# Channel attention on one core: seven packed blocks in place of five, with a shorter ring of row buffers

## The chip, the cores and the metric

The kernel runs on one core of a Trainium2 chip. The metric is device time in microseconds (us). Three runs of the kernel before gave 734.32, 734.56 and 734.57 us; the median, 734.56, is the time before.

## What is computed

The input x is one image of 384 x 384 points with 384 channels in bfloat16, and w1 (384 x 96) and w2 (96 x 384) are small matrices.

```python
xf = x.reshape(B, H * W, C)
gap = jnp.mean(xf, 1)
gmp = jnp.amax(xf, 1)
h_a = gap @ w1;  h_a = h_a * (h_a > 0)
h_m = gmp @ w1;  h_m = h_m * (h_m > 0)
scale = sigmoid(h_a @ w2 + h_m @ w2)
return x * scale[:, None, None, :]
```

Mean and maximum of each channel run over all points, so every point has to be read before the first result can be written. The 113.2 MB of x don't fit into the core's memory. What isn't kept there has to be read a second time.

## The kernel before, in words

A "row" here is one point for each of the 128 partitions: 128 x 384 x 2 bytes = 98,304 bytes (96 KB). The image has TOT = 1152 rows. The kernel divides them into blocks (`take`, from L85 on), and three kinds of block need not be read again:

- **Kept rows.** Three blocks of 44 rows stay in the three slots of `ring` (132 rows), 21 in `held`, 12 in `up`, and a few in PSUM and `acc`.
- **Packed rows.** PACKED = 5 blocks of 32 rows are each packed into 24 rows of `room`. A block has four parts of G = 8 rows: parts 0, 1 and 2 lie in `homes[i]`, part 3 in `fourth[i]`, which is one of two places in `held`.
- **All others** pass through the ring and are read again: `AGAIN`, 800 rows.

**First pass** (loop over `steps`, L317 to L351). SyncE issues the loads in the order of the list `steps`. Each load into the ring goes to the next of three slots, and waits on SyncE's queue until the slot's earlier rows have been used by VectorE (running maximum, L315, in pieces of 6 and 5 rows by HALVES) and by TensorE (sums over the points, L260). All later loads stand behind it. For a packed block ScalarE tests the four parts (L283, L286), TensorE combines them in two halves (L297, 24 matmuls each, into one region of PSUM, `words`), and ScalarE copies each half back (L303, L304). The second half can't start before L304 of the first. In TensorE's order the second half stands after the sums of the first slot that follows the block (`if k == 0`). The list `BETWEEN` gives the loads between two packed blocks, `PASSING` those after the last one, `STAYING`, `LAST_UP` and `LAST_HELD` the pieces of the kept blocks. L347 copies eight early rows into PSUM.

**Between the passes** the scale of each channel is worked out (L355 to L392).

**Second pass.** First the kept rows are multiplied by the scale on VectorE (`multiply`, L397) and stored from ScalarE's queue (`put`). As their stores end, the ring's 132 rows are used as four places of 33 rows, into which SyncE reads blocks of `AGAIN` (`read_into`, L479). Then come 25 turns, counted from 0. Each turn:

1. multiplies a place on VectorE,
2. issues its store from ScalarE (`store`, L473),
3. lets SyncE read the next block into the place as soon as that store has ended,
4. emits a portion of the unpacking (`some`).

The generator `unpack` yields an assumed time for each VectorE instruction: 0.5 for a `tensor_scalar` (L430), 0.9 for `mix` (L434), 1.7 for the multiply of a part, and 0.0 for a byte copy on ScalarE (L440). `some` takes from it until a portion of CHUNK = 4.5 is used up. A block has two halves. Each half has eight VectorE instructions and then six copies on ScalarE; the second half starts by writing the scratch `f`, which the copies of the first half read, and the four multiplies of the block come after all copies. Portions begin in turn 1; blocks 0 to 3 are done by turn 21, block 4 is unpacked in the last turns. Every engine works through its own list in the order of the program, so ScalarE's stores and copies stand in one queue.

Unpacking makes 32 rows of 24, so the fourth part needs a place of its own (`homes_d`): in `held`, `up`, `acc` and in a part of the ring that the last turns don't use. All packed rows are stored in the last turns and after them.

Of the kernel before, what the change touches and what calls it, by code (L numbers as in the profile page):

```python
# [27 lines left out]

SLOT = 44
SLOTS = 3
PLACE = 33
G = 8
PACKED = 5
PSUM_ROWS = 8
LATE_ROWS = 6
BANK_ROWS = 2
# [1 line left out]
HELD_ROWS = 21  # L40
A = 11
HALVES = ((0, 6), (6, 11))
UP_ROWS = 12

FIRST_LOAD = 4
BETWEEN = ((22, 44, 44), (44, 44, 44), (44, 44, 40), (40, 40, 38), (38, 38, 36))
PASSING = (30, 32, 30, 28, 26, 22, 18, 14)
STAYING = ((20, 16, 8), (16, 14, 14), (12, 11, 11, 10))
LAST_UP = (8, 4)
LAST_HELD = (6, 5, 5, 5)  # L50

AGAIN = (33,) * 23 + (24, 17)
FIRST_STORES = ((1, 2, 3, 4, 4, 6, 8, 8, 8), (8, 8, 9, 9, 10), (10, 12, 22))
HELD_STORES = (7, 7, 7)
FIRST_READS = ((8, 8, 8, 9),)
ACC_STORES_AT = 3
EARLY = 4
FROM_TURN = 1
CHUNK = 4.5
TEST_SCALE = 0.031187  # L60
SUM_TAIL = 4
# [4 lines left out]
def kernel(  # L66
# [33 lines left out]
    def take(n):  # L100
        nonlocal at
        at += n
        return at - n, n
# [1 line left out]
    ps_block = take(PSUM_ROWS)  # L105
    beside = take(BANK_ROWS + A)
    packed_block = take(GP * PACKED)
    up_block = take(UP_ROWS)
    held_block = take(sum(LAST_HELD))
    stay = [(take(SLOT), s) for s in range(NS)]  # L110
# [32 lines left out]
    ring = xpool.tile([P, SLOT * NS, C], BF16, name="ring")  # L143
    slots = [ring[:, SLOT * i:SLOT * (i + 1), :] for i in range(NS)]
    places = [ring[:, PLACE * i:PLACE * (i + 1), :] for i in range(SLOT * NS // PLACE)]
    room = xpool.tile([P, 3 * G * PACKED + UP_ROWS, C], BF16, name="room")
    spare = room[:, 3 * G * PACKED, :]
    up = room[:, 3 * G * PACKED:, :]
# [53 lines left out]
    def fill(*parts):  # L202
        nonlocal n_slot
        j = 0
        for block, lo, hi in parts:
            steps.append(("load", block, slots[n_slot % NS][:, j:j + hi - lo, :], lo, hi))
            j += hi - lo
        n_slot += 1

    def whole(block):  # L210
# [19 lines left out]
    turned = []  # L230
    for (block, s), pieces in zip(stay, STAYING):
        s = n_slot % NS
        turned.append((block, s))
        cuts = [sum(pieces[:j]) for j in range(len(pieces) + 1)]
        for lo, hi in zip(cuts, cuts[1:]):
            steps.append(("load", block, slots[s][:, lo:hi, :], lo, hi))
        n_slot += 1
    stay = turned
    for block, buf, pieces in ((up_block, up, LAST_UP), (held_block, held, LAST_HELD)):
# [123 lines left out]
    n = A  # L363
# [9 lines left out]
        acc_pieces.append((lo, hi))  # L373

    def move_late(lo, hi):
        nc.vector.tensor_copy(out=late[:, lo:hi, :].bitcast(U32), in_=up[:, lo:hi, :].bitcast(U32))
        nc.sync.dma_start(out=up[:, lo:hi, :], in_=rows_of(xr, refill)[:, lo:hi, :])

    move_late(0, 2)
    for q0, part_ps in tp_ps:  # L380
# [20 lines left out]
    def put(block, buf, pieces, lo=0):  # L401
        j = 0
        for m in pieces:
            rows = buf[:, j:j + m, :]
            multiply(rows, rows)
            nc.scalar.dma_start(out=rows_of(orr, block)[:, lo + j:lo + j + m, :], in_=rows)
            j += m
# [4 lines left out]
            nc.scalar.dma_start(out=acc_rows(orr, lo, hi), in_=acc[:, lo:hi, :])  # L412


    turns = len(AGAIN)
    beside_last = [places[t % len(places)][:, AGAIN[t]:, :] for t in (turns - 2, turns - 1)]
    homes_d = [held[:, 0:G, :], held[:, G:2 * G, :], up[:, 0:G, :], acc[:, 0:G, :], beside_last[0][:, 0:G, :]]
    HG = G // 2
    f, m = up[:, G:G + HG, :], held[:, 2 * G:2 * G + HG, :]
    t = acc[:, G:G + HG // 2, :].rearrange("p n c -> p (n c)").bitcast(U8)  # L420

    def unpack(i):
# [20 lines left out]
        def nibbles_to_bytes(v):  # L443
            yield scalars(m, v, 3, ALU.logical_shift_right, 0x0101, ALU.bitwise_and)
            yield scalars(m, m, float(0x8F), ALU.mult, 0.0, ALU.add)
            yield mix(v, v, 0x3F3F, ALU.bitwise_xor, ALU.bitwise_xor, m)

        for h in range(2):
            a, b, w, d = (p[:, h * HG:(h + 1) * HG, :] for p in (*(part(i, r) for r in range(3)), homes_d[i]))
            yield scalars(f, w, 4, ALU.logical_shift_right, 0x0F0F, ALU.bitwise_and)  # L450
            yield scalars(w, w, 0x0F0F, ALU.bitwise_and, 0, ALU.bitwise_or)
            yield from nibbles_to_bytes(f)
            yield from nibbles_to_bytes(w)
            yield move(low(d, U8), high(b, U8))
# [6 lines left out]
            multiply(rows, rows)  # L461
            yield 1.7

    def work(blocks):
        for i in blocks:
            yield from unpack(i)

    def some(todo, us):
        while us > 0:
            us -= next(todo, us)  # L470

    def store(buf, block, lo):
        nc.scalar.dma_start(out=rows_of(orr, block)[:, lo:lo + buf.shape[1], :], in_=buf)  # L473
# [17 lines left out]
    (b0, s0), (b1, s1), (b2, s2) = sorted(stay, key=lambda b: b[1])  # L491
    k = ACC_STORES_AT
    put(b0, slots[s0], FIRST_STORES[0][:k])
    put_acc()
    j = sum(FIRST_STORES[0][:k])
    n = SLOT - j
    rest = slots[s0][:, j:, :]
    put(b0, rest, FIRST_STORES[0][k:], j)
    put(held_block, held, HELD_STORES)
    read_into(places[0])  # L500
    put(b1, slots[s1], FIRST_STORES[1])
    put(up_block, up[:, LATE_ROWS:, :], (UP_ROWS - LATE_ROWS,), LATE_ROWS)
    put(refill, up[:, 0:LATE_ROWS, :], (LATE_ROWS,))
    read_into(places[1])
    put(b2, slots[s2], FIRST_STORES[2])
# [4 lines left out]
    early, last = work(range(EARLY)), work(range(EARLY, PACKED))  # L510
    half = 3 * G * 2
    d_at = 3 * G * PACKED
    for turn in range(turns):
        b, buf = order.pop(0)
        multiply(buf[:, 0:b[1], :], buf[:, 0:b[1], :])
        j = turn - (turns - 3)
        if j in (0, 1):
            store(room[:, j * half:(j + 1) * half, :], packed_block, j * half)
        elif j == 2:
            store(held[:, 0:2 * G, :], packed_block, d_at)  # L520
            store(homes_d[2], packed_block, d_at + 2 * G)
            store(homes_d[3], packed_block, d_at + 3 * G)
# [9 lines left out]
    some(last, 1000.0)  # L532
    j = 0
    for block, lo, rows in ((ps_block, 0, kept_ps[:, 0:PSUM_ROWS, :]), (up_block, 0, late), (beside, 0, kept_b)):
        n = rows.shape[1]
        multiply(beside_last[1][:, j:j + n, :], rows)
        store(beside_last[1][:, j:j + n, :], block, lo)
        j += n
    store(homes[4], packed_block, 2 * half)
    store(homes_d[4], packed_block, d_at + 4 * G)  # L540
# [37 lines left out]
```

## Time and profile before

| | |
|---|---|
| Median of three runs | 734.56 us |
| The profiled execution's own time | 733.96 us |
| Its span, first to last instruction | 732.2 us |
| Read from HBM, written | 193.71 MB, 113.25 MB |
| Busy: VectorE, ScalarE, TensorE | 541.4, 247.6, 160.3 us |
| Last maximum of the first pass ends | 271.5 us |
| First multiply by the scale | 277.07 us |
| Turn 0, turn 1, turn 2 start | 315.73, 329.62, 354.11 us |
| Block 0 to 3 unpacked | 336.3 to 550.8 us |
| Turn 22 starts | 654.77 us |

The page of the profile cuts the span into 40 slices of 18.3 us. In a row such as DVE (VectorE) or ACT (ScalarE) a digit is the busy share of a slice in tenths; the row GB/s is what the DMA engines moved. A line of the waits names who waited at which line of the kernel, for whom, and then the microseconds in total, the number of times and the longest. A line of the timeline has the start, the microseconds, engine, line, operation, output<-input, shapes and count, and in brackets the idle time before it with what ended it.

### The profile page before, as it was taken

What the parts mean: (1) busy time and instruction counts of PE and PEld (TensorE: products, weight loads), DVE (VectorE), ACT (ScalarE), POOL (GpSimd) and SP (SyncE); (2) the same over time, 40 slices, a digit from 0 to 9 for tenths busy, and PEclk for the clock granted to TensorE, in tenths of its full rate; (3) what the DMA queues carried; (4) which work ended last, traced back from release to release, by engine and by line L of the source; (5) the groups of instructions that cost most, each with busy time, mean ns of one, the idle gap of its engine ahead of it and who ended that gap; (6) DMA issues with size and microseconds to landing.
All of it is one profiled execution on the core that took longest, in us unless ns stands there. A gap on an engine that the chain in (4) does not pass through costs nothing.

```text
span 732.2 us, 3394 instructions
## 1 busy us (share of the span) xinstructions
PE 160.3 (22%) x1195; PEld 59.9 (8%) x1195; DVE 541.4 (74%) x398; ACT 247.6 (34%) x170; POOL 0.7 (0%) x6
## 2 busy tenths in 40 slices
PE   5375758384654550000000000000000000000000
PEld 1121213131211130000000000000000000000000
DVE  4399999999999999956368869798665543456450
ACT  6969697989200000000251440700530000002700
POOL 0000000000000000000000000000000000000000
PEclk9797979797855555555555555555555555555555
DMA  9999999999999979999999999999999999999997
GB/s 380 436 435 429 422 430 433 426 431 427 417 428 419 422 277 374 398 425 441 428 432 428 432 432 433 431 433 431 433 432 432 435 429 439 428 431 439 432 424 297
DMA packets 21409, 307.18 MB, mean 420 GB/s; under 512 B 2736, under 2 KB 3472, under 8 KB 9616
## 3 DMA queue, kind: packets, MB, share of 16 engines
q1 hardware_dynamic: 12896, 193.71, 62.4%
q10 hardware_dynamic: 8496, 113.25, 36.3%
q8 instruction: 9, 0.15, 0.1%
q14 instruction: 8, 0.07, 0.0%
HBM read 193.71 MB, written 113.25 MB: 419 GB/s over the span
## 4 chain that ended last, share of the span: by engine, by line
DVE 40%; DMA 38%; ACT 12%; issue 4%; PE 1%; ACTq 0%; SPq 0%; DVEq 0%
DMA ring<-in_x_dram 18%; DVE acc L315 16%; DVE ring L397 16%; DMA out_dram<-ring 14%; DMA room<-in_x_dram 5%; ACT room L440 3%; DVE room L397 3%; ACT held L283 2%; DMA held<-in_x_dram 2%; ACT held L286 2%; ACT held L440 2%; ACT acc L440 2%; DVE held L430 1%; DVE held L397 1%; PE kept_ps L297 1%
## 5 line engine op out<-in xcount | busy, mean ns | idle before, releaser
L397 DVE TENSOR_TENSOR ring<-ring,scale_bc 128x12672 bf16<-128x12672 bf16 (+12 forms) x43 | 193.5, 4524 | 81.3 <-DMA ring<-in_x_dram 79.3
L315 DVE TENSOR_TENSOR acc<-acc,ring 128x1920 bf16<-128x1920 bf16 (+4 forms) x184 | 205.4, 1191 | 1.0 <-DMA ring<-in_x_dram 1.0
L260 PE MATMUL bank_a<-ring,small 128*1 128x512 bf16 (+2 forms) x744 | 75.3, 458 | 51.8 <-DMA ring<-in_x_dram 51.8
L397 DVE TENSOR_TENSOR room<-room,scale_bc 128x3072 bf16<-128x3072 bf16 (+1 forms) x18 | 29.9, 1708 | 39.6 <-ACT room L440 39.6
L286 ACT ACTIVATE held<-held 128x3072 uint8<-128x3072 uint8 x20 | 57.1, 2856 | 0.6
L440 ACT COPY ring<-room 128x1536 uint8<-128x1536 uint8 x4 | 5.7, 1473 | 140.8 <-DVE ring L397 140.8
L440 ACT COPY held<-room 128x1536 uint8<-128x1536 uint8 x8 | 11.4, 1472 | 122.3 <-DVE ring L397 122.3
L283 ACT ACTIVATE held<-room,held 128x3072 uint8<-128x3072 int8 x15 | 42.8, 2856 | 23.6 <-DMA room<-in_x_dram 23.3
L440 ACT COPY room<-room 128x1536 uint8<-128x1536 uint8 x24 | 35.0, 1473 | 26.7 <-DVE ring L397 26.4
L260 PEld LDWEIGHTS <-small 128*1 128x1 bf16 x873 | 29.3, 93 | 129.6 <-issue 110.2
L297 PE MATMUL kept_ps<-room,scale_bc 128*128 128x512 fp8e4 (+1 forms) x90 | 30.4, 456 | 39.3 <-ACT room L304 29.1
L440 ACT COPY acc<-room 128x1536 uint8<-128x1536 uint8 x14 | 20.4, 1468 | 42.7 <-DVE ring L397 42.7
L270 ACT COPY w_sb<-bank_a 65x128 f32<-65x128 f32 x2 | 0.5, 262 | 77.6 <-PE bank_a L260 77.1
L315 DVE TENSOR_TENSOR acc<-acc,room 128x1920 bf16<-128x1920 bf16 (+4 forms) x26 | 26.5, 1078 | 0.0
L430 DVE TENSOR_SCALAR room<-room 128x1536 uint16<-128x1536 uint16 x20 | 11.2, 558 | 18.3 <-ACT room L440 17.9
L297 PE MATMUL kept_ps<-room,w_sb 128*128 128x512 fp8e3 (+1 forms) x60 | 21.1, 439 | 0.0
L297 PE MATMUL kept_ps<-held,room 128*128 128x512 fp8e4 (+1 forms) x60 | 19.9, 417 | 0.0
L434 DVE SCALAR_TENSOR_TENSOR room<-room,held 128x768 uint32<-128x768 uint32 x20 | 19.2, 958 | 0.7
L303 ACT COPY room<-room 128x1536 uint8<-128x1536 uint8 x10 | 14.7, 1468 | 2.7 <-PE kept_ps L297 2.7
L440 ACT COPY room<-acc 128x1536 uint8<-128x1536 uint8 x10 | 14.7, 1474 | 0.3
L260 PE MATMUL bank_a<-room,small 128*1 128x512 bf16 x99 | 10.7, 456 | 18.3 <-DMA room<-in_x_dram 18.3
L303 ACT COPY room<-held 128x1536 uint8<-128x1536 uint8 x10 | 14.7, 1470 | 0.0
(65 smaller groups left out, 155.0 us busy)
## 6 DMA issues: line engine op xcount, KB each, us to landing
out_dram<-ring ACTq DMA_DIRECT2D x23, 3168.0 KB, 25.6
ring<-in_x_dram SPq DMA_DIRECT2D x22, 3168.0 KB, 26.2
ring<-in_x_dram SPq DMA_DIRECT2D x7, 4224.0 KB, 21.9
ring<-in_x_dram SPq DMA_DIRECT2D x3, 3840.0 KB, 22.3
ring<-in_x_dram SPq DMA_DIRECT2D x3, 3648.0 KB, 22.7
room<-in_x_dram SPq DMA_DIRECT2D x4, 2304.0 KB, 27.6
out_dram<-room ACTq DMA_DIRECT2D x2, 4608.0 KB, 39.1
ring<-in_x_dram SPq DMA_DIRECT2D x2, 2880.0 KB, 15.1
```

The costliest lines, as they stand in the source:

```text
L260: nc.tensor.matmul(sum_ps[q * QP:q * QP + 1, 0:g * P], lhsT=ones_bf[:, 0:1], rhs=rows[:, k:k + g, q * P:(q + 1) * P], start=(done + k == 0 ...
L270: nc.scalar.copy(out=s_sb[r % 2], in_=sum_ps[:, r * P:(r + 1) * P])
L283: nc.scalar.activation(out=tested, in_=high(part(i, r), I8), func=ACT.Square, bias=test_bias, scale=TEST_SCALE,)
L286: nc.scalar.activation(out=tested, in_=tested, func=ACT.Square, bias=minus4, accum_out=tests[:, 4 * i + r:4 * i + r + 1],)
L297: nc.tensor.matmul(words[:, c:c + BANK], lhsT=weights[2 * r + k], rhs=high(part(i, r), dt)[:, half * n + c:half * n + c + BANK], start=(r ...
L303: nc.scalar.copy(out=high(part(i, r), U8)[:, span], in_=low(part(i, r + 2), U8)[:, span])
L315: nc.vector.tensor_tensor(out=out_, in0=in0, in1=in1, op=ALU.max)
L397: nc.vector.tensor_tensor(out=dst, in0=src, in1=scale_bc.unsqueeze(1).to_broadcast([P, n, C]), op=ALU.mult)
L430: nc.vector.tensor_scalar(out=u16(dst), in0=u16(src), scalar1=s1, scalar2=s2, op0=op0, op1=op1)
L434: nc.vector.scalar_tensor_tensor(out=u32(dst), in0=u32(src), scalar=both(s), in1=u32(other), op0=op0, op1=op1)
L440: nc.scalar.copy(out=dst, in_=src)
```

## The change

- PACKED goes from 5 to 7. `room` keeps 3 x 8 x 7 = 168 rows; `up` is gone, and the refilled rows of the first pass's end now lie at the start of `held`.
- The ring has 96 rows in place of 132. In the first pass it has three slots of 31 rows (the block kept in the last slot has 34), in the second four places of 24 rows.
- `BETWEEN` has four loads between two packed blocks, of 26 or 27 rows (10 for the first). The second half of a packed block's matmuls stands after the second of them (`if k == 1`). Three passing blocks follow in place of eight.
- 784 rows are read again, in 33 turns.
- Unpacking begins in turn 0 and takes all seven blocks with the same portions of 4.5. Blocks 0 and 1 are stored as soon as each is unpacked. After block 1, its home of 24 rows is used as a fifth place of the ring.
- Four more `homes_d` lie in places that were used before: block 2's in `held` 0 to 8, which held block 1's, block 3's in `held` 8 to 16, which held block 0's, and those of blocks 5 and 6 in block 0's home. From block 2 on the scratch `f` lies there too.

```diff
-SLOT = 44
+SLOT = 31
+RING = 96
-PLACE = 33
+PLACE = 24
-PACKED = 5
+PACKED = 7
-BETWEEN = ((22, 44, 44), (44, 44, 44), (44, 44, 40), (40, 40, 38), (38, 38, 36))
-PASSING = (30, 32, 30, 28, 26, 22, 18, 14)
-STAYING = ((20, 16, 8), (16, 14, 14), (12, 11, 11, 10))
-LAST_UP = (8, 4)
+BETWEEN = ((10, 27, 27, 27),) + ((26, 26, 26, 26),) * 6
+PASSING = (26, 23, 20)
+STAYING = {1: (16, 15), 2: (13, 11, 10), 0: (9, 8, 7, 7)}
-AGAIN = (33,) * 23 + (24, 17)
-FIRST_STORES = ((1, 2, 3, 4, 4, 6, 8, 8, 8), (8, 8, 9, 9, 10), (10, 12, 22))
-HELD_STORES = (7, 7, 7)
-FIRST_READS = ((8, 8, 8, 9),)
+AGAIN = (24,) * 32 + (16,)
+FIRST_STORES = ((1, 2, 3, 4, 5, 5, 5, 6), (8, 8, 8, 7), (9, 11, 14))
+HELD_STORES = (7, 8)
+FIRST_READS = ((6, 6, 6, 6),)
-EARLY = 4
-FROM_TURN = 1
...
-            if k == 0:
+            if k == 1:
                 steps.append(("pack", i, 1))
...
-    homes_d = [held[:, 0:G, :], held[:, G:2 * G, :], up[:, 0:G, :], acc[:, 0:G, :], beside_last[0][:, 0:G, :]]
+    homes_d = [held[:, G:2 * G, :], held[:, 0:G, :], held[:, 0:G, :], held[:, G:2 * G, :], acc[:, 0:G, :]]
+    homes_d += [room[:, 0:G, :], room[:, G:2 * G, :]]
...
+        f = room[:, 2 * G:2 * G + HG, :] if i > 1 else acc[:, 0:HG, :]
...
-    def work(blocks):
-        for i in blocks:
+    def work():
+        for i in range(PACKED):
             yield from unpack(i)
+            if i < 2:
+                store(homes[i], packed_block, 3 * G * i)
+                store(homes_d[i], packed_block, d_at + G * i)
+            if i == 1:
+                read_into(homes[1])
...
+    after = [
+        [(room[:, step:2 * step, :], step)],
+        [(room[:, 2 * step:3 * step, :], 2 * step)],
+        [(held[:, 0:2 * G, :], d_at + 2 * G), (homes_d[4], d_at + 4 * G), (room[:, 0:2 * G, :], d_at + 5 * G)],
+    ]
     for turn in range(turns):
         b, buf = order.pop(0)
         multiply(buf[:, 0:b[1], :], buf[:, 0:b[1], :])
...
+        if turn >= turns - len(after):
+            for rows, lo in after[turn - turns + len(after)]:
+                store(rows, packed_block, lo)
         store(buf[:, 0:b[1], :], b, 0)
         read_into(buf)
-        if FROM_TURN <= turn < turns - 4:
-            some(early, CHUNK)
-        elif turn == turns - 4:
-            some(early, 1000.0)
-        elif turn > turns - 4:
-            some(last, CHUNK)
+        if turn == turns - 4:
+            last = buf
+        some(todo, CHUNK if turn < turns - len(after) - 1 else 1000.0)
```

More of the change, by code (lines that the diff above doesn't have):

```diff
@@ L42 @@
 HALVES = ((0, 6), (6, 11))
-UP_ROWS = 12
 FIRST_LOAD = 4
-BETWEEN = ((22, 44, 44), (44, 44, 44), (44, 44, 40), (40, 40, 38), (38, 38, 36))
-PASSING = (30, 32, 30, 28, 26, 22, 18, 14)
-STAYING = ((20, 16, 8), (16, 14, 14), (12, 11, 11, 10))
-LAST_UP = (8, 4)
+BETWEEN = ((10, 27, 27, 27),) + ((26, 26, 26, 26),) * 6
+PASSING = (26, 23, 20)
+STAYING = {1: (16, 15), 2: (13, 11, 10), 0: (9, 8, 7, 7)}
 LAST_HELD = (6, 5, 5, 5)
-AGAIN = (33,) * 23 + (24, 17)
-FIRST_STORES = ((1, 2, 3, 4, 4, 6, 8, 8, 8), (8, 8, 9, 9, 10), (10, 12, 22))
-HELD_STORES = (7, 7, 7)
-FIRST_READS = ((8, 8, 8, 9),)
+AGAIN = (24,) * 32 + (16,)
+FIRST_STORES = ((1, 2, 3, 4, 5, 5, 5, 6), (8, 8, 8, 7), (9, 11, 14))
+HELD_STORES = (7, 8)
+FIRST_READS = ((6, 6, 6, 6),)
 ACC_STORES_AT = 3
-EARLY = 4
-FROM_TURN = 1
 CHUNK = 4.5
@@ L107 @@
     packed_block = take(GP * PACKED)
-    up_block = take(UP_ROWS)
     held_block = take(sum(LAST_HELD))
-    stay = [(take(SLOT), s) for s in range(NS)]
+    stay = {s: take(sum(pieces)) for s, pieces in STAYING.items()}
     refill = take(LATE_ROWS)
@@ L142 @@
     held = nc.alloc_sbuf_tensor_at("held", [P, HELD_ROWS, C], BF16, offset=RING_BYTES).ap()
[L143 to L148, printed above, removed]
+    ring = xpool.tile([P, RING, C], BF16, name="ring")
+    slots = [ring[:, SLOT * i:SLOT * i + stay[i][1], :] for i in range(NS)]
+    places = [ring[:, PLACE * i:PLACE * (i + 1), :] for i in range(RING // PLACE)]
+    spare = ring[:, SLOT * NS, :]
+    room = xpool.tile([P, 3 * G * PACKED, C], BF16, name="room")
     homes = [room[:, 3 * G * i:3 * G * (i + 1), :] for i in range(PACKED)]
@@ L207, in fill @@
             j += hi - lo
+            assert j <= SLOT
         n_slot += 1
@@ L229 @@
     fill(whole(refill), whole(passing[-1]))
[L230 to L239, printed above, removed]
+    assert n_slot % NS == next(iter(stay))
+    parts_left = [(stay[i], slots[i], pieces) for i, pieces in STAYING.items()] + [(held_block, held, LAST_HELD)]
+    for block, buf, pieces in parts_left:
         for j, m in enumerate(pieces):
@@ L375, in move_late @@
     def move_late(lo, hi):
-        nc.vector.tensor_copy(out=late[:, lo:hi, :].bitcast(U32), in_=up[:, lo:hi, :].bitcast(U32))
-        nc.sync.dma_start(out=up[:, lo:hi, :], in_=rows_of(xr, refill)[:, lo:hi, :])
+        nc.vector.tensor_copy(out=late[:, lo:hi, :].bitcast(U32), in_=held[:, lo:hi, :].bitcast(U32))
+        nc.sync.dma_start(out=held[:, lo:hi, :], in_=rows_of(xr, refill)[:, lo:hi, :])
     move_late(0, 2)
@@ L415 @@
     turns = len(AGAIN)
-    beside_last = [places[t % len(places)][:, AGAIN[t]:, :] for t in (turns - 2, turns - 1)]
-    homes_d = [held[:, 0:G, :], held[:, G:2 * G, :], up[:, 0:G, :], acc[:, 0:G, :], beside_last[0][:, 0:G, :]]
+    homes_d = [held[:, G:2 * G, :], held[:, 0:G, :], held[:, 0:G, :], held[:, G:2 * G, :], acc[:, 0:G, :]]
+    homes_d += [room[:, 0:G, :], room[:, G:2 * G, :]]
     HG = G // 2
-    f, m = up[:, G:G + HG, :], held[:, 2 * G:2 * G + HG, :]
+    m = held[:, 2 * G:2 * G + HG, :]
     t = acc[:, G:G + HG // 2, :].rearrange("p n c -> p (n c)").bitcast(U8)
@@ L462, in unpack @@
             yield 1.7
-    def work(blocks):
-        for i in blocks:
+    d_at = 3 * G * PACKED
+    def work():
+        for i in range(PACKED):
             yield from unpack(i)
+            if i < 2:
[3 more added lines that the diff above has]
+                read_into(homes[1])
     def some(todo, us):
@@ L489, in read_into @@
             order.append((b, buf))
-    (b0, s0), (b1, s1), (b2, s2) = sorted(stay, key=lambda b: b[1])
     k = ACC_STORES_AT
-    put(b0, slots[s0], FIRST_STORES[0][:k])
+    put(stay[0], slots[0], FIRST_STORES[0][:k])
     put_acc()
     j = sum(FIRST_STORES[0][:k])
[L496 to L499, printed above, removed]
+    put(stay[0], slots[0][:, j:, :], FIRST_STORES[0][k:], j)
+    put(held_block, held[:, LATE_ROWS:, :], HELD_STORES, LATE_ROWS)
+    put(refill, held[:, 0:LATE_ROWS, :], (LATE_ROWS,))
     read_into(places[0])
-    put(b1, slots[s1], FIRST_STORES[1])
-    put(up_block, up[:, LATE_ROWS:, :], (UP_ROWS - LATE_ROWS,), LATE_ROWS)
-    put(refill, up[:, 0:LATE_ROWS, :], (LATE_ROWS,))
+    put(stay[1], slots[1], FIRST_STORES[1])
     read_into(places[1])
-    put(b2, slots[s2], FIRST_STORES[2])
+    put(stay[2], slots[2], FIRST_STORES[2])
     read_into(places[2])
@@ L509 @@
     bad = nc.values_load(flag, engines=(ENG.SP, ENG.Activation, ENG.DVE))
-    early, last = work(range(EARLY)), work(range(EARLY, PACKED))
-    half = 3 * G * 2
-    d_at = 3 * G * PACKED
+    todo = work()
+    step = 3 * G * 2
+    after = [
[3 more added lines that the diff above has]
+    ]
     for turn in range(turns):
@@ L515 @@
         multiply(buf[:, 0:b[1], :], buf[:, 0:b[1], :])
[L516 to L522, printed above, removed]
+        if turn >= turns - len(after):
+            for rows, lo in after[turn - turns + len(after)]:
+                store(rows, packed_block, lo)
         store(buf[:, 0:b[1], :], b, 0)
         read_into(buf)
-        if FROM_TURN <= turn < turns - 4:
-            some(early, CHUNK)
-        elif turn == turns - 4:
-            some(early, 1000.0)
-        elif turn > turns - 4:
-            some(last, CHUNK)
+        if turn == turns - 4:
+            last = buf
+        some(todo, CHUNK if turn < turns - len(after) - 1 else 1000.0)
     assert not again and not order
-    some(last, 1000.0)
     j = 0
-    for block, lo, rows in ((ps_block, 0, kept_ps[:, 0:PSUM_ROWS, :]), (up_block, 0, late), (beside, 0, kept_b)):
+    for block, lo, rows in ((ps_block, 0, kept_ps[:, 0:PSUM_ROWS, :]), (held_block, 0, late), (beside, 0, kept_b)):
         n = rows.shape[1]
-        multiply(beside_last[1][:, j:j + n, :], rows)
-        store(beside_last[1][:, j:j + n, :], block, lo)
+        multiply(last[:, j:j + n, :], rows)
+        store(last[:, j:j + n, :], block, lo)
         j += n
-    store(homes[4], packed_block, 2 * half)
-    store(homes_d[4], packed_block, d_at + 4 * G)
+    store(homes[PACKED - 1], packed_block, 3 * G * (PACKED - 1))
     with tc.If(bad != 0):
```

## The prediction

> **What bounds the kernel now.** I read the slices first, then the waits, then VectorE's and ScalarE's timelines, turn by turn.
>
> ```profile
> DVE  4399999999999999956368869798665543456450
> ACT  6969697989200000000251440700530000002700
> ...
> GB/s 380 436 435 429 422 430 433 426 431 427 417 428 419 422 277 374 398 425 441 428 432 428 432 432 433 431 433 431 433 432 432 435 429 439 428 431 439 432 424 297
> ```
>
> The transfers are the bound almost everywhere: some 430 GB/s outside the turn between the passes. In the first pass VectorE is full too. In the second it is half empty on average, which hides this:
>
> ```profile
> DVE ring L397 <- DMA ring<-in_x_dram: 79.3, 11, 12.4
> ...
> DVE room L397 <- ACT room L440: 39.6, 5, 9.1
> ...
> DVE room L430 <- ACT room L440: 17.9, 5, 5.0
> ```
>
> While a block is unpacked VectorE also waits for ScalarE's byte copies: 57.5 us for five blocks. Three turns in the timeline of VectorE:
>
> ```profile
> 354.11 6.76 DVE L397 TENSOR_TENSOR ring<-ring,scale_bc 128x12672 bf16<-128x12672 bf16 x1 [12.43 <-DMA ring<-in_x_dram]
> 365.82 1.16 DVE L430 TENSOR_SCALAR room<-room 128x1536 uint16<-128x1536 uint16 x2 [4.95 <-ACT room L440]
> ...
> 371.13 6.75 DVE L397 TENSOR_TENSOR ring<-ring,scale_bc 128x12672 bf16<-128x12672 bf16 x1
> 386.94 5.09 DVE L397 TENSOR_TENSOR room<-room,scale_bc 128x3072 bf16<-128x3072 bf16 x3 [9.05 <-ACT room L440]
> 391.95 6.75 DVE L397 TENSOR_TENSOR ring<-ring,scale_bc 128x12672 bf16<-128x12672 bf16 x1
> ```
>
> A turn is the multiply of one place (6.75 us for 33 rows), then a portion of unpacking. The second turn here lasts 391.95 - 371.13 = 20.8 us, although nothing in it waits for a transfer. Turns that only wait for transfers (starts at 564.82 to 654.77, six of them) are 14.99 us apart: 66 rows read and written, **0.2271 us a row**. From 354.11 to 504.82 ten turns took 150.7 us with one DMA wait of 2.0: without it 14.87 each. So VectorE with ScalarE is just level with the transfers while it unpacks. Later there is slack.
>
> In the first pass I look at the load queue and at packing block 1:
>
> ```profile
> 2.11 2.44 SPq L329 DMA_DIRECT2D ring<-in_x_dram  x5
> ...
> 39.93 19.02 SPq L329 DMA_DIRECT2D ring<-in_x_dram  x3
> ```
>
> ```profile
> 47.41 2.86 ACT L283 ACTIVATE held<-room,held 128x3072 uint8<-128x3072 int8 x1 [5.74 <-DMA room<-in_x_dram]
> ...
> 67.63 1.44 ACT L304 ACTIVATE room<-kept_ps 128x1536 uint16<-128x1536 f32 x1
> ...
> 77.56 1.44 ACT L304 ACTIVATE room<-kept_ps 128x1536 uint16<-128x1536 f32 x1
> ```
>
> ScalarE needs 47.41 to 79.0 = **31.6 us a block**. A block's share of the loads is now 160 to 164 rows, over 35 us; ScalarE idles 5.7 to 5.9 us ahead of blocks 1 and 2. The load queue stands from 4.6 to 39.9 us, until the first slot is free, and lives on 195 rows issued before.
>
> **The change, step by step** (all against the profiled span, 732.2 us; that run took 733.96, so 1.76 lie outside; the median is 734.56, 0.6 above it).
>
> *Rows not read again.* 800 becomes 784: 16 x 0.2271 = **-3.6 us** where the transfers bound. Writes stay 1152 rows.
>
> *Unit counts in the first pass.* By the loop over HALVES the maxima go from 224 to 230; a 6-row and a 5-row one take 1.35 and 1.15 us, 0.2 a row and under 0.15 fixed: +0.5 to +0.9 us, hidden if the transfers end last.
>
> *Queue depth, first pass.* Only 32+31+27+27 = 117 rows are issued at the start (195 before); they last to about 30 us. Slot 0 is free when VectorE has finished it: it waits for L304 until 30.1 as now (14.5 us in the waits), and 10 rows in place of 22 make the release some 2.5 us earlier than 39.93: 37.4. So the transfers stand some 8 us. Read alone they ran at 441 GB/s (40 to 55 us), 0.223 a row; the 51 rows to the end of packed block 1's first part land at 37.4 + 2 + 11.4 = 50.7.
>
> *ScalarE, first pass.* A block now has 32 + 104 rows = 30.3 us of transfers against 31.6 of ScalarE, so ScalarE falls behind by 1.3 a block. Block 6 starts at 50.7 + 5 x 31.6 = 208.7. TensorE's second half of a block ended 28.7 us after ScalarE's start (block 1: 76.1 - 47.4), here at 237.4, and TensorE works in order, so the third slot's sums stand behind it: 1.9 us, 239.3. That slot takes the 23-row load. Without that wait it would be issued before 233 (all before it has landed at about 235). After it come 166 rows: 239.3 + 2 + 37.0 = 278.3 for the last landing and 1.2 more for the last maximum: 279.5, against 270.38 + 1.16 = 271.5 now. **+8 us**. Bounds: 0 (the stand at 30 us is made up at 0.223 a row) and +10 (166 rows at the 421 GB/s of 210 to 240 us).
>
> *Start of the second pass.* The 176 kept rows took 277.07 to 313.95, in 25 multiplies; 128 rows in 21 take 27.1. Scale ready at 285.1, kept rows done 312.2, turn 0 at 313.9 (the same 1.7 behind). Turn 1's place is read once 87 kept rows are stored: first store 287.5, then 87 + 24 rows, then 24 read beside as many written, 159 rows x 0.2271 = 36.1, landing 2: about **326**.
>
> *The turns.* The units of 0.5, 0.9 and 1.7 are dealt out in portions of 4.5 as before, so portions 0 to 12 are those of the trace, one turn earlier, and blocks 4 to 6 repeat portions 3 to 12 (a block ends in portion 2, 12 and 22 with one multiply over). Turn lengths in the trace: portion 0: 12.1 without its DMA wait; 1: 17.0; 2: 20.8; 3 to 12: 391.95 to 542.37 less 2.0 of DMA wait = 148.4; 13: 8.3. A 24-row multiply (128x9216, in the trace) takes 4.96, 1.80 less. Turn 1 to turn 24 are portions 1 to 23: 17.0 + 20.8 + 148.4 + 148.4 + 8.3 = 342.9 less 23 x 1.80 = 41.3: **301.6 us**. The transfers would need 23 x 48 x 0.2271 = 250.7. The waits for ScalarE don't shrink: its six copies (8.6 us) start when the store behind the multiply is issued, whatever the multiply's length, and end before the next one does. So **VectorE with ScalarE becomes the bound**. The 64 packed rows stored on the way and the fifth place take up part of the gap.
>
> *A new wait.* Block 2's copies go to held 0 to 8, where block 1's fourth part is being stored. That store is issued at the end of block 1's multiplies; the first such copy comes 1.7 + 4.96 + 0.4 = 7.0 us later. Ahead of it are some 16 rows of turn 6's store and 24 of block 1's, with its own 8: 48 rows alone are 10.9 + 2 to land, with reads between some 16. Behind the copy wait ScalarE's later copies and the store of turn 8, and VectorE. Bounds 0 and 19 (a 33-row store lands in 25.6). Nearest are the 768 KB stores (8.8) and the 2304 KB one (20.4) : 15 less 7 = **+8 us**.
>
> *The end.* Turn 24 starts at 326 + 301.6 + 8 = 635.6. Not yet issued then: 8 x 24 + 16 + 160 + 16 = 384 rows to write, 88 to read; in flight 46 (turn 23's store and read): 518 x 0.2271 = 117.6, with all engines ahead. The same count in the trace at turn 22 (654.77): 250 + 78 = 328 rows, 74.5 us, 729.3, and the span ends 2.9 later. So 635.6 + 117.6 + 2.9 = **756.1**, with 1.76: **758 us**.
>
> The smaller pieces themselves I cost at nothing: 33-row transfers lasted 26 us each and still ran at 432 GB/s, since others lay beside them. The Trainium skill, "DMA: Bandwidth & Descriptors", section "Anatomy of one DMA", gives a fixed 2.0 us to each DMA besides its bytes, which speaks against 24-row pieces: unhidden, 16 more transfers would be an estimated 32 us more. The trace disagrees with paying it each time: two 33-row transfers would then need over 18 us a turn, and a turn took 14.99.
>
> **The rivals.**
> - *One of the two late terms is hidden* (first pass or the new wait): **750**; both: 742. For it: the first pass lost little at the same place in block 4 (421 GB/s). Against: there 164-row blocks left ScalarE idle.
> - *Second pass bound by transfers, first pass late*: 733.96 + 8 - 3.6 = **738**.
> - *The other side: the transfers bound both passes.* ScalarE's copies fall under VectorE's ring multiplies and its tests keep up with the loads. A block's 3.43 turns now cost VectorE 17.5 of work (12 x 0.56, 4 x 0.96, 4 x 1.75), 57.5 / 5 = 11.5 of waits and 3.43 x 4.96 = 17.0 of multiplies, 46; its transfers need 3.43 x 10.9 + 2.9 (64 + 24 rows over seven blocks) = 40.3. From 6 us less of the waits on the transfers bound: 733.96 - 3.6 = **730**. For it: the DMA row is full in every second-pass slice now. Against: the turns of 17 and 21 us, at an unchanged copy length.
> - *Each transfer pays a start of its own.* Bounded from above by the smallest stores, which land 4.3 us after their issue (96 KB): 16 more transfers, up to 69 us, over 768. Against: 26 us transfers lie side by side now, and two of 33 rows fit into 14.99.
>
> **How the numbers follow.** The measurement tells about 0.2%, 1.5 us (733.1 to 736.0). Chances: forecast, 752 to 766, 0.60; one or both terms hidden, 742 to 752, 0.19; 738, 0.07; 730, 0.08; between them, about no change, 0.03; above 768, 0.03, of it 0.01 for the start of each transfer. So faster 0.08, same 0.04, slower 0.88. The range leaves out 730 to 738 and the top: 740 to 768.
>
> **What would show it.** First pass: GB/s falls in the second slice; the 23-row load issued near 239; scale some 8 us later. Second: turns 13 us long on average, VectorE above 90% with waits for L440 from turn 1 to 24, GB/s under 410 there, a ScalarE wait of some 8 us for a store in block 2, then 432 GB/s to the end. Wrong if the turns are near 11 us, or if the second-pass slices stay at 430.

## The result and the profile after

The changed kernel takes 784.32 us (median of four runs, 783.41 to 785.12) against 734.44 us for the kernel before, measured beside it: a ratio of 1.068, 95% interval 1.0662 to 1.0699. It was forecast slower, at 758 us with a range of 740 to 768. The direction was right, the size was half of what came, and the time lies outside the range. The profiled execution took 783.41 us with a span of 781.6.

First the slices of the changed kernel (19.5 us each; VectorE, ScalarE, transfers):

```profile
DVE  4499999999997999745959069758697858934300
ACT  7859999999994000034170170444444061000000
...
GB/s 382 225 426 426 431 427 427 431 422 430 430 426 332 420 243 381 430 415 434 389 431 400 432 333 332 396 362 350 282 393 345 413 379 373 407 435 430 439 418 367
```

Three places have lost transfers: the second slice (225), the thirteenth (332), and everything from slice 24 to slice 34, 282 to 413 GB/s where the kernel before ran at 430. (The 243 of the fifteenth is the stretch between the passes, which the kernel before has too, with 277.) Over longer windows, with the busy time of each engine and at the end of the line the GB/s, first the changed kernel while it unpacks, then the kernel before while it does:

```profile
core 0: us, PE busy (x) PEld busy (x) DVE busy (x) ACT busy (x) POOL busy (x), PEclk, DMA share, GB/s
339.00:659.00 320.00, 0.00 (x0) 0.00 (x0) 225.60 (x156) 119.59 (x84) 0.00 (x0) 0.50 0.94 380
```

```profile
330.00:551.00 221.00, 0.00 (x0) 0.00 (x0) 161.27 (x95) 68.34 (x48) 0.00 (x0) 0.50 1.01 432
```

That gives the whole bill. At 380 instead of 432 GB/s, 320 us hold 320 x (1 - 380/432) = 38.5 us without transfers. The scale is ready 14.5 us later (first multiply at 291.57 against 277.07). The rows that aren't read again give back 3.6. 38.5 + 14.5 - 3.6 = 49.4, and the spans differ by 781.6 - 732.2 = 49.4 us. (Outside these windows both second passes lose nearly the same: against 432 GB/s for their 1952 and 1936 rows, some 11 us each.)

The waits of the changed kernel (L386 is the multiply that was L397, L430 the copy that was L440, L420 the `tensor_scalar` that was L430):

```profile
DVE room L386 <- ACT room L430: 51.9, 7, 9.1
...
ACT held L430 <- DMA out_dram<-held: 37.2, 1, 37.2
DVE room L420 <- ACT room L430: 32.8, 5, 19.8
...
DVE ring L386 <- DMA ring<-in_x_dram: 27.0, 6, 6.0
...
DVE acc L420 <- ACT room L430: 7.3, 2, 4.7
```

VectorE's waits for ScalarE rose from 57.5 to 92.0 us (51.9 + 32.8 + 7.3), its waits for read rows fell from 79.3 to 27.0: the sign that the bound has moved from the transfers to VectorE with ScalarE. The line of 37.2 us is new. Here are the turns around it in VectorE's timeline, and ScalarE's at the same time:

```profile
412.67 4.95 DVE L386 TENSOR_TENSOR ring<-ring,scale_bc 128x9216 bf16<-128x9216 bf16 x1
...
422.41 4.95 DVE L386 TENSOR_TENSOR ring<-ring,scale_bc 128x9216 bf16<-128x9216 bf16 x1
...
450.76 1.16 DVE L420 TENSOR_SCALAR room<-room 128x1536 uint16<-128x1536 uint16 x2 [19.76 <-ACT room L430]
...
452.30 4.95 DVE L386 TENSOR_TENSOR ring<-ring,scale_bc 128x9216 bf16<-128x9216 bf16 x1
```

```profile
420.99 0.34 ACTq L471 DMA_DIRECT2D out_dram<-held  x1
427.39 0.34 ACTq L471 DMA_DIRECT2D out_dram<-ring  x1
446.51 2.85 ACT L430 COPY held<-room 128x1536 uint8<-128x1536 uint8 x2 [37.22 <-DMA out_dram<-held]
```

Block 1's fourth part, eight rows, is given to the store queue at 420.99. ScalarE could copy for block 2 from 427.7 on and stands until 446.5, when that store has ended. VectorE stands 19.8 us for the copies behind it. Turn 7 lasts 29.89 us; its portion took 12.96 in the kernel before, 11.16 after taking off what the shorter multiply saves. The other turns came as they were laid out from the old trace: portions 2 to 6 were to last 19.02, 9.66, 12.74, 17.35 and 9.74 us, and turn starts at 353.91, 372.92, 382.58, 395.32, 412.67 and 422.41 give 19.01, 9.66, 12.74, 17.35 and 9.74.

In the first pass, the load queue and VectorE at the start, ScalarE's starts of blocks 1, 5 and 6, and the load queue and VectorE after the last block:

```profile
2.11 35.04 SPq L318 DMA_DIRECT2D ring<-in_x_dram  x6
```

```profile
30.47 1.76 DVE L336 COPY kept_ps<-ring 128x1536 uint32<-128x1536 uint32 x1 [14.51 <-ACT room L293]
```

```profile
51.63 2.86 ACT L272 ACTIVATE held<-room,held 128x3072 uint8<-128x3072 int8 x1 [8.42 <-DMA room<-in_x_dram]
...
179.63 2.84 ACT L272 ACTIVATE held<-room,held 128x3072 uint8<-128x3072 int8 x1
...
211.26 2.84 ACT L272 ACTIVATE held<-room,held 128x3072 uint8<-128x3072 int8 x1
```

```profile
241.04 5.42 SPq L318 DMA_DIRECT2D ring<-in_x_dram  x5
```

```profile
240.42 5.64 DVE L304 TENSOR_TENSOR acc<-acc,ring 128x1920 bf16<-128x1920 bf16 x5 [0.31 <-DMA ring<-in_x_dram]
250.27 12.98 DVE L304 TENSOR_TENSOR acc<-acc,ring 128x2304 bf16<-128x2304 bf16 x13 [4.21 <-DMA ring<-in_x_dram]
```

Until 30.5 us VectorE's copy of the early rows into PSUM waited for ScalarE, so slot 0 came free late: of the six ring loads in the first line, the sixth was issued only at 36.8 us. From 30 to 40 us the transfers ran at 62 GB/s. Block 1's tests start at 51.6 (47.4 before). From block 2 on ScalarE no longer waits for loads: blocks 5 and 6 start 31.6 us apart, back to back. TensorE's second half of block 6 ran until 239.6 us, and the sums of the third slot came right behind it. The 23-row load, which takes that slot, was issued at 241.04, and VectorE stood 4.2 us until it landed.

### The profile page after: what moved, and what is told of

Its sections match the earlier page's. It is cut to its first block, busy times and chain, and to the rows that moved or that the text cites. A ratio compares the mean times of both kernels' runs of the same rounds, so it can differ in the third digit from the quotient of the medians.

```text
span 781.6 us, 3821 instructions
## 1 busy us (share of the span) xinstructions
PE 182.6 (23%) x1321; PEld 70.0 (9%) x1321; DVE 564.3 (72%) x448; ACT 343.8 (44%) x230; POOL 0.7 (0%) x6
## 4 chain that ended last, share of the span: by engine, by line
DVE 40%; ACT 23%; DMA 21%; issue 5%; PE 4%; ACTq 1%; SPq 0%; DVEq 0%
DVE ring L386 16%; DMA ring<-in_x_dram 11%; DVE acc L304 10%; DVE room L386 7%; ACT room L430 7%; DMA out_dram<-ring 5%; ACT held L272 4%; PE kept_ps L286 3%; DMA out_dram<-held 3%; ACT held L275 3%; ACT held L430 3%; ACT room L292 3%; DVE held L420 2%; ACT acc L430 2%; DVE room L420 1%
## 5 line engine op out<-in xcount | busy, mean ns | idle before, releaser
L386 DVE TENSOR_TENSOR ring<-ring,scale_bc 128x9216 bf16<-128x9216 bf16 (+12 forms) x43 | 157.5, 3687 | 27.3 <-DMA ring<-in_x_dram 27.0
L386 DVE TENSOR_TENSOR room<-room,scale_bc 128x3072 bf16<-128x3072 bf16 (+1 forms) x28 | 64.0, 2325 | 58.6 <-ACT room L430 51.9
L430 ACT COPY held<-room 128x1536 uint8<-128x1536 uint8 x12 | 17.3, 1473 | 156.5 <-DVE ring L386 92.2
L249 PE MATMUL bank_a<-ring,small 128*1 128x512 bf16 (+2 forms) x735 | 72.1, 447 | 50.8 <-DMA ring<-in_x_dram 50.5
L275 ACT ACTIVATE held<-held 128x3072 uint8<-128x3072 uint8 x28 | 80.0, 2856 | 0.9
L430 ACT COPY room<-room 128x1536 uint8<-128x1536 uint8 x32 | 46.4, 1473 | 54.9 <-DVE ring L386 27.4
L272 ACT ACTIVATE held<-room,held 128x3072 uint8<-128x3072 int8 x21 | 59.9, 2853 | 13.8 <-DMA room<-in_x_dram 13.4
L420 DVE TENSOR_SCALAR room<-room 128x1536 uint16<-128x1536 uint16 x24 | 13.4, 559 | 33.2 <-ACT room L430 32.8
L430 ACT COPY acc<-room 128x1536 uint8<-128x1536 uint8 x18 | 26.2, 1468 | 24.2 <-DVE ring L386 24.2
L304 DVE TENSOR_TENSOR acc<-acc,room 128x2304 bf16<-128x2304 bf16 (+2 forms) x33 | 34.3, 1103 | 0.0
L286 PE MATMUL kept_ps<-room,w_sb 128*128 128x512 fp8e3 x84 | 29.7, 441 | 0.0
L286 PE MATMUL kept_ps<-held,ring 128*128 128x512 fp8e4 x84 | 27.5, 411 | 0.0
L430 ACT COPY room<-acc 128x1536 uint8<-128x1536 uint8 x18 | 26.5, 1473 | 0.4
L292 ACT COPY room<-room 128x1536 uint8<-128x1536 uint8 x14 | 20.5, 1466 | 5.2 <-PE kept_ps L286 5.1
L293 ACT ACTIVATE room<-kept_ps 128x1536 uint16<-128x1536 f32 x14 | 20.2, 1440 | 0.0
L272 ACT ACTIVATE held<-held 128x3072 uint8<-128x3072 int8 x7 | 19.9, 2843 | 0.0
## 6 DMA issues: line engine op xcount, KB each, us to landing
out_dram<-room ACTq DMA_DIRECT2D x8, 2304.0 KB, 19.8
```

The costliest lines, as they stand in the source:

```text
L249: nc.tensor.matmul(sum_ps[q * QP:q * QP + 1, 0:g * P], lhsT=ones_bf[:, 0:1], rhs=rows[:, k:k + g, q * P:(q + 1) * P], start=(done + k == 0 ...
L272: nc.scalar.activation(out=tested, in_=high(part(i, r), I8), func=ACT.Square, bias=test_bias, scale=TEST_SCALE,)
L275: nc.scalar.activation(out=tested, in_=tested, func=ACT.Square, bias=minus4, accum_out=tests[:, 4 * i + r:4 * i + r + 1],)
L286: nc.tensor.matmul(words[:, c:c + BANK], lhsT=weights[2 * r + k], rhs=high(part(i, r), dt)[:, half * n + c:half * n + c + BANK], start=(r ...
L292: nc.scalar.copy(out=high(part(i, r), U8)[:, span], in_=low(part(i, r + 2), U8)[:, span])
L293: nc.scalar.activation(out=part(i, 2).rearrange("p n c -> p (n c)").bitcast(U16)[:, span], in_=words, func=ACT.Copy, bias=32767.5,)
```

## The experiments

Each is compared with the kernel before, measured beside it (733.4 to 733.8 us). The theory: the second pass is bound by the chain of VectorE and ScalarE, with one long wait for a store in it, and the first pass is late through the early hole and through TensorE's order behind ScalarE's last block. The rivals are that transfers bound it anyway, or that the shorter ring does harm by itself.

**1. Without the wait for the store.** The fourth parts of blocks 0 and 1 change places, so block 2 copies to where block 0's was stored long before.

```diff
-    homes_d = [held[:, G:2 * G, :], held[:, 0:G, :], held[:, 0:G, :], ...
+    homes_d = [held[:, 0:G, :], held[:, G:2 * G, :], held[:, 0:G, :], ...
```

> The changed kernel with one edit: block 0's fourth part goes to held 0 to 8 and block 1's to held 8 to 16, so that block 2's copies go where block 0's part was stored 40 us earlier, and not where block 1's is just being stored. Theory A (VectorE with ScalarE bounds the unpacking, and the 18.7 us by which the turn behind turn 7 is longer than its portion's length in the trace of before, 29.9 against 11.2, is lost): turn 24 starts some 18 us earlier and the time falls from 784 to 765 to 769. Rival B (the transfers ran at 400 to 432 GB/s during that wait and are the real bound): 780 to 784.

Measured: 765.03 us, ratio 1.0426 (1.0407 to 1.0446). Theory A. Turn 7 lasts 434.35 - 423.19 = 11.16 us, to the hundredth the length laid out for it. 19.3 us of the 49.9 are this one wait, though transfers ran at 430 GB/s while ScalarE stood (427.7 to 446.5 us): they worked off what was queued, and fell to 339 GB/s in the 20 us behind it.

**2. Other VectorE work beside the copies.** With the swap of experiment 1; each half of a block gets its own scratch, and a block's multiplies come after the first half of the next block.

```diff
-        f = room[:, 2 * G:2 * G + HG, :] if i > 1 else acc[:, 0:HG, :]
         for h in range(2):
+            f = room[:, 2 * G + h * HG:2 * G + (h + 1) * HG, :] if i > 1 else acc[:, h * HG:(h + 1) * HG, :]
...
             yield from nibbles_to_bytes(w)
+            if h == 0:
+                yield from finish(i - 1)
             yield move(low(d, U8), high(b, U8))
```

(`finish` holds the four multiplies and the two early stores of the block given to it.)

> The changed kernel with block 0's and 1's fourth parts swapped as in the first experiment, a scratch of its own for each half of a block, and the four multiplies of a block moved behind the first half of the next block's VectorE work, so that ScalarE's copies have other VectorE work beside them. All work is kept. Theory A (VectorE's waits for the copies, 11.5 us a block, make it the bound): the waits for the copies fall under 25 us in total, turns 1 to 24 take 260 to 275 us in place of 320, the second pass runs at 425 GB/s or more and the time is 742 to 750. Rival B (places of 24 rows can't keep the transfers full, whatever VectorE does): turns stay over 12.5 us with waits for transfers, 760 or more.

Measured: 748.57 us, ratio 1.0215 (1.0178 to 1.0252). Turns 1 to 24 take 339.91 to 607.34 = 267.4 us in place of 319.9. In the windows of this kernel, with the same VectorE and ScalarE work as above:

```profile
340.00:607.00 267.00, 0.00 (x0) 0.00 (x0) 225.22 (x155) 119.41 (x84) 0.00 (x0) 0.50 1.00 427
```

The work is unchanged (225 us and 119 us busy), only its order differs, and the transfers run at 427 GB/s. Of VectorE's waits for the copies, 73.2 us in experiment 1, one of 9.1 us is left:

```profile
DVE room L420 <- DMA out_dram<-room: 16.5, 1, 16.5
...
DVE room L386 <- ACT room L430: 9.1, 1, 9.1
```

This is theory A. So 24-row places can keep the transfers full, and the waits for the copies were the loss. A new wait came in with it, 16.5 us for the store of block 0's home, where block 2's scratch lies; experiment 8 takes it up.

**3. The second half of the packing one slot later**, behind the third slot's sums.

```diff
-            if k == 1:
+            if k == 2:
                 steps.append(("pack", i, 1))
```

> The changed kernel with the second half of a packed block's matmuls placed after the sums of the third slot that follows, not of the second. In the changed kernel the 23-row load after the last block was issued at 241.0 us, behind the third slot's sums, which stood behind block 6's second half. Theory A (that wait costs the first pass its late end): the load is issued 6 to 9 us earlier, VectorE doesn't stand from 246 to 250, the first multiply by the scale comes at 284 to 287 in place of 291.6, the time is 776 to 780. Rival B (VectorE's own work or the early hole in the loads sets the end of the first pass): 290 to 292 and 783 to 785.

Measured: 777.71 us, ratio 1.0606 (1.0585 to 1.0626): 6.6 us less. The load queue and VectorE at the same place in this kernel:

```profile
234.88 12.25 SPq L318 DMA_DIRECT2D ring<-in_x_dram  x5
```

```profile
241.09 21.93 DVE L304 TENSOR_TENSOR acc<-acc,ring 128x1920 bf16<-128x1920 bf16 x21 [0.32 <-DMA ring<-in_x_dram]
```

The 23-row load is issued at 234.88 in place of 241.04, 6.2 us earlier, and VectorE runs on behind the block before it where it stood 4.2 us. The first multiply by the scale comes at 287.94, 3.6 us earlier, a little less than expected; the time is in theory A's range. (Experiments 1, 2 and 6 have the changed kernel's first pass, and their first multiplies come at 292.10 to 293.47, so its own 291.57 is the earliest of four; profiles of one first pass differ by up to 1.9 us.) VectorE works for the last 35.8 us without a break in both kernels.

**4. The early hole.** The PSUM tile `kept_ps` is cut in two.

```diff
-    kept_ps = psum.tile([P, PSUM_ROWS + G, C], BF16)
-    late = kept_ps[:, G:G + LATE_ROWS, :]
-    words = kept_ps[:, G:, :].rearrange(...)
+    kept_ps = psum.tile([P, PSUM_ROWS, C], BF16)
+    words_ps = psum.tile([P, G, C], BF16)
+    late = words_ps[:, 0:LATE_ROWS, :]
+    words = words_ps.rearrange(...)
```

> The changed kernel with the PSUM tile that holds eight kept rows and the words of the packing cut into two tiles. VectorE's copy of the kept rows then has nothing in common with ScalarE's read of the words, for which it waited 14.5 us. Theory A (the hole at 30 to 40 us, 62 GB/s, comes from that wait through slot 0, and it shifts ScalarE's chain of seven blocks, which then sets the late load): the hole goes, block 1's tests start at 43 to 45 in place of 51.6, the scale comes 6 to 8 us earlier, the time is 776 to 779. Rival B (made up later in the pass): the hole goes and the time stays at 783 to 785.

Measured: 774.33 us (770.56 to 776.78), ratio 1.0568 (1.0544 to 1.0592): 10 us less, somewhat more than expected. VectorE's wait of 14.5 us is gone. From 30 to 40 us the transfers run at 419 GB/s, and the start of block 1 in ScalarE's timeline is

```profile
43.56 2.85 ACT L273 ACTIVATE held<-room,held 128x3072 uint8<-128x3072 int8 x1 [3.14 <-DMA room<-in_x_dram]
```

8.1 us earlier than in the changed kernel. The first multiply by the scale comes 7.5 us earlier, at 284.07. So the hole is not made up later, because ScalarE works through its blocks back to back from there. The profiled run, at 770.56 us the fastest of its four, is 12.8 us shorter than that of the changed kernel: 7.5 from here, 2.9 between the first multiply and turn 1, and 2.4 from VectorE's wait behind block 1's store (17.4 in place of 19.8). Whether the edit caused the last two is not shown.

**5. Smaller places alone**, in the kernel before: five places of 24 rows.

```diff
-PLACE = 33
-AGAIN = (33,) * 23 + (24, 17)
-FIRST_READS = ((8, 8, 8, 9),)
+PLACE = 24
+AGAIN = (24,) * 31 + (16, 16, 16, 8)
+FIRST_READS = ((6, 6, 6, 6),)
```

> The kernel before with five places of 24 rows in the second pass in place of four of 33; five packed blocks and the first pass as before. Theory A (24-row turns leave less time beside each portion of unpacking: 13.0 us a turn against 10.9 of transfers while four blocks are unpacked): turns 1 to 15 need some 181 us against 153 of transfers, less what the places hold ahead: 748 to 756. Rival B (place size doesn't matter, the loss is the seven blocks' own): 734 to 738.

Measured: 742.39 us, ratio 1.0124 (1.0106 to 1.0143), between the two. The turns came as theory A has them, 322.51 to 505.92 = 183.4 us for turns 1 to 15. But the loss is smaller than its 14 to 22 us:

```profile
322.00:506.00 184.00, 0.00 (x0) 0.00 (x0) 136.34 (x95) 68.34 (x48) 0.00 (x0) 0.50 0.99 415
```

415 in place of 432 GB/s over 184 us are 7.2 us. A chain that is slower than its transfers costs only from the moment at which the queued transfers are used up; here the transfers ran at 429 GB/s up to 444 us, and the loss shows in slices 25 to 28 alone (381 GB/s from 444 to 518 us). With seven blocks the chain lasts 320 us, and most of its surplus is paid.

**6. Smaller portions:** the unpacking is spread over 28 turns in place of 24.

```diff
-CHUNK = 4.5
+CHUNK = 3.6
```

> The changed kernel with portions of 3.6 in place of 4.5: the same unpacking is dealt out over turns 0 to 27 in place of 0 to 23. Theory A (a turn is too long for its transfers, so spreading the same VectorE chain over four more turns gives back some 4 x (10.9 - 5.0) = 24 us of transfers): 758 to 768, block 2's wait kept. Rival B (the chain itself, not its spread, sets the end, or the waits grow with more cuts): 780 to 790.

Measured: 768.80 us, ratio 1.048 (1.0449 to 1.0511): 15.5 us less, in theory A's direction and just short of its range. The cuts fall elsewhere, and some waits grew: VectorE's multiplies waited 56.1 us for copies (51.9), and ScalarE stood 40.3 us for the store of block 1's fourth part (37.2). The spread's share can't be told apart from these, so the 24 us are neither shown nor refuted.

**7. Everything together** (experiments 1 to 4 in one kernel).

> All edits of the other experiments but the portions: parts swapped, second scratch and later multiplies, second half of the packing after the third slot, PSUM tile cut in two. Theory A (the four causes add up and nothing else is lost): the first pass ends within 3 us of the kernel before (271.5), the second is bound by its transfers: 728 to 736. Rival B (the shorter ring costs transfers by itself): 742 or more.

Measured: 733.83 us, ratio 0.9992 (0.9978 to 1.0007). Theory A: the four causes take back 784.3 - 733.8 = 50.5 us. One by one they gave 19.3, then 16.5 on top of it, 6.6 and 10.0: 52.4. The scale comes at 279.21 us, 2.1 after that of the kernel before, and from 340 to 610 us the transfers run at 429 GB/s. With seven blocks and a ring of 96 rows the kernel is level with the one before.

**8. The scratch of blocks 2 and 3 in `acc`**, in the kernel of experiment 7, where VectorE still stood 16.1 us for a store:

```profile
393.43 1.15 DVE L421 TENSOR_SCALAR room<-room 128x1536 uint16<-128x1536 uint16 x2 [16.05 <-DMA out_dram<-room]
```

```diff
-            f = room[:, 2 * G + h * HG:...] if i > 1 else acc[:, h * HG:(h + 1) * HG, :]
+            f = room[:, 2 * G + h * HG:...] if i > 3 else acc[:, h * HG:(h + 1) * HG, :]
```

> The kernel with all edits, and the scratch of blocks 2 and 3 in the accumulator's rows like that of blocks 0 and 1, not in block 0's home. In the kernel with all edits VectorE stood 16.1 us behind turn 5, because block 2's scratch was written where block 0's home was still being stored. Theory A (the transfers bound the second pass there and the places hold enough ahead, so that this wait cost little): the wait goes and the time moves by 0 to 2 us, 732 to 734 by the same runs of before. Rival B (a stand of that length costs transfers, as block 2's wait did in the changed kernel): 8 to 16 us less, 718 to 726.

Measured: 730.95 us, ratio 0.9977 (0.9966 to 0.9989). The wait is gone, and the time is 2.9 us below experiment 7's by the medians, 1.1 by the ratios, whose intervals overlap: theory A within the noise, and far from rival B. In place of the store VectorE now waits longer for read rows (66.2 us in place of 55.2). A stand of nearly the same length cost 19 us in the changed kernel and 1 to 3 here: there the chain was the bound, here the transfers are, and they had work queued. This version is 0.23% below the kernel before (interval 0.11 to 0.34%) and, by the medians, 6.8% below the changed kernel.

**9. The packing one slot later still** (`k == 3`), in the kernel of experiment 8.

> The kernel of the run beside it, with the second half of the packing after the fourth slot's sums instead of the third's. Theory A (after the third slot TensorE's order no longer holds up a slot): within 1 us of it. Rival B (slots are still released late by TensorE, which is the 2 us by which the first pass still ends later than in the kernel before): 2 to 4 us less.

Measured: 731.65 us, ratio 0.9982 (0.9972 to 0.9992): within 1 us of experiment 8. TensorE's order is used up as a cause. Why the first pass still ends 1.6 us later than in the kernel before (scale at 278.72 in experiment 8 and 278.64 here, against 277.07) stays open.

**10. The cut PSUM tile in the kernel before.**

> The kernel before with the PSUM tile cut in two as in the other experiment: VectorE doesn't stand 14.5 us at the start. Theory A (VectorE's backlog of 14.5 us bounds the first pass of the kernel before, though the loads ran on from 132 rows of slots): the first pass ends 3 to 8 us earlier, 727 to 731. Rival B (the transfers bound it): 733 to 735.

Measured: 734.16 us, ratio 1.0021 (0.9992 to 1.005). My theory falls: VectorE no longer stands 14.5 us at the start, and nothing is gained. It now waits for loads instead:

```profile
30.55 9.44 DVE L316 TENSOR_TENSOR acc<-acc,ring 128x2304 bf16<-128x2304 bf16 x8 [5.03 <-DMA ring<-in_x_dram]
```

The last maximum of the loads ends at 271.4, against 271.5. There the first pass is bound by its transfers; VectorE's full row in the slices was backlog, not bound. The same edit is worth 10 us in the changed kernel, whose shorter slots ran dry during that stand.

## Why the prediction was wrong, step by step

- **What becomes the bound: right.** The turns of the unpacking came out as laid out from the old trace, and experiments 1 and 2 show that the chain of VectorE and ScalarE sets the second pass. Turns 1 to 24 without the new wait: 319.9 - 18.7 = 301.2 us against 301.6 predicted.
- **The new wait: the mechanism right, the size wrong. This is the step that failed most, 10.3 us of the 25.5 below.** "+8 us" became 29.89 - 11.16 = 18.7. I had put its landing at 15 us, from bounds 0 and 19 for the wait. The store landed 446.51 - 420.99 = 25.5 us after its issue. Some 16 rows of turn 6's store and reads for a few microseconds were to lie ahead of it. But from that store's issue (417.65) to the landing the transfers moved some 28.9 x 0.412 / 0.0983 = 121 rows at 412 GB/s, and the stores up to it hold 56. So over half was for something else: reads, the store issued behind it, and what was left of earlier ones. A busy pair of queues decided this wait, not the rows of the store; the 33-row stores' 25.6 us, taken for the upper end, was the right row. The 8.8 us of the 768 KB stores was the wrong one. The old page has more rows of that size:

```profile
out_dram<-ring ACTq DMA_DIRECT2D x7, 768.0 KB, 8.8
...
out_dram<-room ACTq DMA_DIRECT2D x1, 768.0 KB, 33.0
out_dram<-acc ACTq DMA_DIRECT2D x1, 768.0 KB, 34.4
```

Five of the seven in the first line are stores of kept rows before the turns (median 5.2 us by the trace), the other two were issued later and had a median of 18.1. So the row mixes two stages, and every store of this size issued in the turns or after them took some 18 us or more.

- **Late first pass: the chain right, the last stretch too short.** Block 6 was to start at 208.7 (211.3), the 23-row load to be issued at 239.3 (241.0). But the load landed 9.1 us after its issue where I took 7.1. The 166 rows, its own 23 and 143 behind them, then kept VectorE busy from 250.3 to 286.0 without a break, where I let the transfers set the end. So +14.5 came in place of +8: 1.7 from the issue, 2.0 from the landing, 2.8 from VectorE's last stretch. Experiments 3 and 4 show both halves of the mechanism.
- **Start of the second pass: too short.** From the first multiply to turn 0 were 31.6 us (28.8 predicted) and on to turn 1 15.8 (12.1): the first places landed later, and VectorE waited 3.8 and 5.6 us for them. No experiment took this by itself; in the kernel of experiment 7 the two stretches still last 30.8 and 15.6 us, so the cause stays open.
- **The end: right to 2 us.** From turn 24 (658.86) to the end of the span 122.7 us against 120.5.

The errors sum to 6.5 (first pass) + 2.8 + 3.7 (turns 0 and 1) + 10.3 (new wait, less 0.4 of shorter turns) + 2.2 = 25.5 us, and 756.1 + 25.5 = 781.6. All have one sign. The new wait was taken below the middle of its bounds (8 of 0 to 19) and came at the top; the late first pass was taken at 8 of 0 to 10 and passed its upper bound; the start of the second pass had no bounds. The range then held a single term's upper bound, not several at once.

Of the rivals, *the transfers bound both passes* and *second pass bound by transfers* are refuted by the turns and the 380 GB/s, and *one late term is hidden* by experiments 1, 3 and 4. *A start of its own for each transfer* is refuted by experiments 2 and 8, where the same 24-row transfers run at 427 and 431 GB/s. The Trainium skill, "DMA: Bandwidth & Descriptors", section "Anatomy of one DMA — SWDGE (gpsimd) path", gives the fixed part of about 2.0 us per DMA for transfers that GpSimd issues, while SyncE and ScalarE issue them here. Paid once per queued transfer it would make a turn of one read and one store of 24 rows an estimated 14.8 us by that page's fit; such a turn of experiment 2 took 10.9 us (559.92 to 570.82), so the trace disagrees with paying it each time.

## What to carry to other kernels

An engine at half load on average can be the bound of a stage: lay out its waits in the order of the program, and hold the length of one turn against the transfers of one turn. A buffer that is used again right after its store is issued can cost the length of the store queue, not of the store (25.5 us here for eight rows); read such a price from rows of the same stage, and give such reuse to the oldest buffer. When ring slots get shorter, every stand that the longer slots covered comes back as a cost, so count the microseconds of transfers that are already issued when an engine is known to stop.

## What was not expected of the hardware

- A store of eight rows (768 KB) took 25.5 us to land behind two busy queues. In the kernel before, five stores of that size ahead of the turns had a median of 5.2, and four later ones took 18.1 (median of two), 33.0 and 34.4.
- When the load queue had run dry, the next load of 23 rows landed 9.1 us after its issue, though 23 rows at 430 GB/s are 5.3. In these 9.1 us the transfers moved 344 GB/s, 32 rows' worth, so part of the time went to loads issued behind it.
- The same 14.5 us stand of VectorE on one PSUM tile cost nothing with 195 rows of loads issued ahead, and 10 us with 117.
